# Attention and MLP in one pipeline: transposes of P and the scores moved to the second half of TensorE's slot, with ScalarE's order to match

## Chip, core and metric

The kernel runs on one core of a Trainium2 chip. The metric is the device time of one execution in microseconds. Before the change it is 1642.52 us, the median of three runs (1642.33 to 1642.61). The engines are called PE (TensorE; PEld is its weight load), ACT (ScalarE), DVE (VectorE), POOL (GpSimd) and SP (the engine that issues most DMAs).

## What is computed

Attention in which each row of scores keeps its 32 largest entries, for 8 batches, 8 heads, 576 tokens and a head size of 64; its output, laid out as 4608 tokens by 512, goes through a two-layer MLP with exact gelu. All in fp32.

```python
scores = scale * np.matmul(q, k.transpose(0, 1, 3, 2))
kth = np.partition(scores, -top_k, axis=-1)[..., -top_k:-top_k + 1]
scores = np.where(scores >= kth, scores, -1000000000.0)
scores = scores - np.max(scores, axis=-1, keepdims=True)
attn = np.exp(scores)
attn = attn / (np.sum(attn, axis=-1, keepdims=True) + 1e-09)
x = np.matmul(attn, v)            # then (B,H,S,D) -> (B*S, H*D)
h = x @ w_in                      # 512 -> 2048
g = 0.5 * h * (1.0 + erf(h * inv_sqrt2))
out = g @ w_out                   # 2048 -> 512
```

The weights arrive as 8-byte words, which the kernel turns into fp32 itself in its first slots.

## The kernel before

Instructions are issued to each engine in the order in which the program writes them; no scheduler moves them. So the order is that of one loop, `for n in range(ahead)`, one pass of which is a **slot**. An **item** is 128 rows of scores of two heads (a "pair" of heads); there are 144, 18 to a batch, and the two last row groups of 64 are joined from two pairs ("last" items). The parts of one item are spread over six slots: in slot n the program issues

- `attend(n - 3)` (L509, L520): the product o of the transposed P and v, in every second slot (a **first-layer slot**, by the MLP work that falls into it; the others are **second-layer slots**), and in each slot for last items. Its copy to `xT` on ACT (L514, L524) is put in a list and issued by `copy_x`.
- `softmax(n - 1, e)` for both heads e (L403, L404): a Prelu that pushes entries below the threshold far down, then an exp with its row sum. `add_small` (L396, POOL) follows it.
- `transposes(n - 2)` (L445): 16 transposes of P into two PSUM buffers and two copies `pt` (L457).
- `scores(n + 2)` (L290, L304) with the copy to `s` (L298, L309), and `last_keys(n + 2)` (L323, L331) with the tail transposes of item n - 2 (L462, L467) and their copies (L463, L474, L342, L344).
- `top_k(n)` on DVE (L364, L369): four rounds of eight maxima for both heads. In the third round stands `inverse(n - 1)` (L390), the reciprocal of the row sum, so DVE's top-k of item n can't end before the softmax of item n - 1 has. Then `normalise(n - 1)` (L416, POOL, in some weight slots DVE) and `threshold(n)` (L379, L382, POOL), which gives the next softmax its `neg` and `bias`.
- eight **pieces** of the MLP (`mlp`): a piece is four records of 128x256 matmuls for the first layer (L561, `h_ps`) or two of 128x512 for the second (L597, `y_ps`). Blocks of eight pieces alternate between both layers. The gelus (L572) of a first-layer block are due behind the piece with index `GELU_AT` of the next second-layer block, and are issued at the next `run_gelus()`. A piece is ready only when its tokens are (`ready`): where it isn't, the slot is a **border**, at four slots in every 36.
- pieces of `transpose_qk` (L246): three per pair, of four, two and four transposes of q and k blocks, each with a copy `qk` (L250). The third issues the loads of the pair after next on SP. Slots are given out by `slots_of` and `prep_in`.

Exp and gelu belong to different function tables of ACT; the compiler puts a table load wherever the order changes from one to the other.

PSUM has two buffers with the tag `tp`, taken in turn by everything that is transposed and by o: `tp_qk`, both `tp`, `t_ps`, `o`. `h_ps` has two, `y_ps` two, the scores' `s_ps` one of two banks.

In slots 1 to 10 and 13 to 18 a unit of the weights is made: two or three casts on ACT (L175, L177, L179) at the end of the slot before, sums on POOL (L198, L210, in the later ones also L195). MLP work begins in slot 10 (`START`); before it PE is kept busy with warm matmuls (L675).

Of the kernel before, what the change touches and what calls it, by code (L numbers as in the profile page):

```python
# [14 lines left out]
def kernel(  # L15
# [108 lines left out]
    START = 2 * NP + 2  # L124
# [46 lines left out]
    def weights_size(u):  # L171
        if u not in words:
            return
        w, first, below, d = parts(u)
        nc.scalar.activation(d, first, func=AF.Relu, bias=low, scale=2.0**19)  # L175

        nc.scalar.activation(below, first, func=AF.Prelu, bias=high, scale=2.0**-21, alpha=2.0**40)  # L177
        if not on_pool(u):
            nc.scalar.activation(w.bitcast(i32), w.bitcast(u32), func=AF.Copy, scale=2.0**-13)  # L179

    def on_pool(u):

        return u in words and SLOT_OF[u] > START

    def waits(u):

        return u == ORDER[-1]
# [3 lines left out]
    def weights_add(u):  # L191
        if u in words:
            w, _, below, d = parts(u)
            if on_pool(u):
                nc.gpsimd.tensor_scalar(  # L195
                    w.bitcast(i32), w.bitcast(u32), 2.0**-13, None, op0=ALU.mult
                )
            nc.gpsimd.tensor_tensor(d, d, below, op=ALU.add)  # L198
            if not ends_late(u):
                weights_end(u)  # L200
        made.add(u)

    def ends_late(u):

        return u in words and SLOT_OF[u] <= START

    def weights_end(u):
        if u in words:
            w, _, _, d = parts(u)
            nc.gpsimd.tensor_tensor(d, d, w.bitcast(i32), op=ALU.add)  # L210


    items, starts = [], []
# [20 lines left out]
    def transpose_qk(pair, first=False):  # L234

        rq, rk = raw_of("q", pair), raw_of("k", pair)
        blocks = [(rq, j) for j in range(NJ)] + [(rk, NM)] + [(rk, j) for j in range(NM)]

        def piece(c, n):
            if pair not in qk_of:  # L240
                qk_of[pair] = work.tile([P, KT + SM], f32, tag="qk", bufs=NP + 2, name="qk")
            t = qk_of[pair]
            tp = ps.tile([P, 512], f32, tag="tp", name="tp_qk")
            for x in range(n):
                r, j = blocks[c + x]
                nc.tensor.transpose(  # L246
                    tp[:, x * P : (x + 1) * P], r[:, j].rearrange("p e d -> p (e d)"), ident
                )
            copy = nc.vector.tensor_copy if first and c > 0 else nc.scalar.copy
            copy(out=t[:, c * P : (c + n) * P], in_=tp[:, 0 : n * P])  # L250
            if c == 0:
                load("q", pair + 2)
                load("k", pair + 2)

        return [lambda c=c, n=n: piece(c, n) for c, n in ((6, 4), (4, 2), (0, 4))]
# [5 lines left out]
    def row(i, e):  # L261
        return S_of[i][:, e * S : (e + 1) * S]
# [111 lines left out]
    def threshold(i):  # L374

        if i < 0 or i >= N:
            return
        st = stat_of[i]
        nc.gpsimd.tensor_scalar(  # L379
            st["neg"], st["top"][:, :, 0 :: TOPK - 1], -1.0, None, op0=ALU.mult  # L380
        )
        nc.gpsimd.tensor_tensor(  # L382
            st["bias"], st["neg"][:, :, 0], st["neg"][:, :, 1], op=ALU.subtract
        )

    def inverse(i):
        if i < 0 or i >= N:
            return
        st = stat_of[i]
        nc.vector.reciprocal(st["rden"], st["den"])  # L390

    def add_small(i):
        if i < 0 or i >= N:
            return
        st = stat_of[i]
        nc.gpsimd.tensor_scalar(st["den"], st["den"], 1e-9, None, op0=ALU.add)  # L396

    def softmax(i, e):

        if i < 0 or i >= N:  # L400
            return
        st, s = stat_of[i], row(i, e)
        nc.scalar.activation(s, s, func=AF.Prelu, bias=st["neg"][:, e, 1:2], scale=1.0, alpha=STEEP)  # L403
        nc.scalar.activation(  # L404
            s, s, func=AF.Exp, bias=st["bias"][:, e : e + 1], scale=1.0,
            accum_out=st["den"][:, e : e + 1],
        )

    def normalise(i, on_dve):

        if i < 0 or i >= N:
            return
        st = stat_of[i]
        for e in range(2):
            s = row(i, e)
            (nc.vector if e >= 2 - on_dve else nc.gpsimd).tensor_scalar(  # L416
                s, s, st["rden"][:, e : e + 1], None, op0=ALU.mult
            )
# [64 lines left out]
    def copy_x():  # L483
        while copies:
            copies.pop()()

    n_tok, read = [0], [0]
# [80 lines left out]
    def gelus(us):  # L568
        for u in us:
            _, n, _, nf = units[u]  # L570
            g_of[u] = work.tile([P, nf, n], f32, tag="g", bufs=4, name="g")
            nc.scalar.activation(g_of[u], h_of.pop(u), func=AF.Gelu)  # L572
# [45 lines left out]


    pieces = []  # L620
    GELU_AT = 5

    def block(u, first):

        do, need = (l1_piece, units[u][0] + units[u][1]) if first else (l2_piece, 0)
        return [(need, lambda w=w, x=x: do(w, x)) for w in (u, u + 1) for x in range(4)]
# [3 lines left out]
    def behind(work, x, us):  # L630
        need, f = work[x]
        work[x] = need, lambda: (f(), waiting.append(us))
        return work

    def run_gelus():
        while waiting:
            gelus(waiting.pop(0))

    pieces += behind(block(0, True), 7, (0, 1)) + block(2, True)
    for u in range(2, NU, 2):  # L640
        pieces += behind(block(u - 2, False), GELU_AT, (u, u + 1))
        if u + 2 < NU:
            pieces += block(u + 2, True)
    pieces += block(NU - 2, False)
    done = [0]

    def mlp(n):
        for _ in range(n):
            if done[0] >= len(pieces) or pieces[done[0]][0] > ready[0] or left[0] == 0:
                return  # L650
            pieces[done[0]][1]()
            done[0] += 1
            left[0] -= 1
            if eager[0]:
                run_gelus()


    ready, left = [0], [0]
# [13 lines left out]
    def keep_busy(count, m):  # L672
        warm = ps.tile([P, 512], f32, tag="l1", name="warm")
        for _ in range(count):
            nc.tensor.matmul(warm[:, 0:P], lhsT=m, rhs=m, start=True, stop=True)  # L675
# [17 lines left out]
    prep_in = {}  # L693
    for pair in range(2, n_pairs):
        b, p = divmod(pair, NP)
        for at, piece in zip(first.get(pair, slots_of[b % 2][p]), transpose_qk(pair)):
            prep_in.setdefault(starts[b] + at, []).append(piece)
    ahead = N + 4
    for n in range(ahead):

        left[0] = 4 if n in (START, START + 1) else 8
        eager[0] = n > N
        if not waits(unit_in(n)):
            weights_add(unit_in(n))
        product = attend(n - 3)
        late = n > START
        copy_x()
        for e in range(2):
            softmax(n - 1, e)
        add_small(n - 1)  # L710
        if waits(unit_in(n)):
            weights_size(unit_in(n))
            weights_add(unit_in(n))
        mlp(1 if product else 3)
        if n < START:

            keep_busy((4 if product or n == 0 else 14) * (1 if n < 5 else 2), ident)

        tails = transposes(n - 2)
        scores(n + 2)  # L720
        ready[0] = n_tok[0]
        prep = prep_in.pop(n, [])
        if n == START + 1:

            for piece in prep:
                piece()
            prep = []
        if n < START and product:
            keep_busy(5 if n < 5 else 10, ident)
        mlp(4)  # L730
        last_keys(n + 2, tails)
        if ends_late(unit_in(n)):
            weights_end(unit_in(n))
        for piece in prep:
            mlp(1)
            piece()
        if n == 1:
            keep_busy(8, ident)

        run_gelus()  # L740
        mlp(left[0])
        run_gelus()
        u = unit_in(n + 1)
        if n < N:
            top_k(n, {2: lambda: inverse(n - 1)})
        else:
            inverse(n - 1)

        normalise(n - 1, 2 if on_pool(u) else 0)
        threshold(n)  # L750

        if not waits(unit_in(n + 1)):
            weights_size(unit_in(n + 1))
        for m in (n + 1, n + 2):

            if m > 2 and waits(unit_in(m)) == (m == n + 1):
                load_weights(m)
        if n <= NP:
            load("v", n)
# [38 lines left out]
```

## Time and profile before

| | |
|---|---|
| median of three runs | 1642.52 us |
| the profiled execution | 1642.62 us |
| its span, first to last instruction | 1640.9 us |
| PE matmul busy | 1589.6 us |
| DVE busy | 1412.3 us |
| ACT busy | 1179.4 us |
| POOL busy | 665.4 us |
| mean granted TensorE clock | 0.993 |

The busy time of PE is that of its records, whose ends are modelled, so a wait of PE shows better in the chain and in the waits than in this share. In a line of the waits the columns are: who waited, for whom, us in total, times, longest. In a line of the chain: start, us, what. In a line of the timeline: start, us, engine, line, operation, and in brackets the engine's idle time before it and what ended that. In a line of the stages: busy time of PE, PEld, DVE, ACT and POOL with the number of instructions, then the granted clock, the DMA share and GB/s.

### The profile page before, as it was taken

The page shows a single profiled execution, that of the slowest core. Times are in us where ns is not written, and L with a number is a line of the kernel's source. Part 1 is how long each engine was busy: PE and PEld are TensorE (multiplying, and loading weights), DVE is VectorE, ACT ScalarE, POOL GpSimd, SP SyncE. Part 2 cuts the span into 40 slices and gives each one's busy share as a digit, 9 for nine tenths or more (in the row PEclk, how much of TensorE's full clock was granted, in tenths as well). Part 3 has the DMA queues.
Part 4 walks back from the last instruction along what each step waited for, and adds up shares of the span by engine and source line. Part 5 has one row for each costly group of instructions (what it writes and reads, how often), then busy time and mean ns, then how long its engine had stood idle before and what let it go on. Part 6 is the DMA issues. An engine that isn't in the chain of part 4 may idle for free.

```text
span 1640.9 us, 27895 instructions
## 1 busy us (share of the span) xinstructions
PE 1589.6 (97%) x10336; PEld 1059.6 (65%) x10336; DVE 1412.3 (86%) x3046; ACT 1179.4 (72%) x2132; POOL 665.4 (41%) x760
## 2 busy tenths in 40 slices
PE   7888999999999999999999999999999999999999
PEld 6766566766666666666666656676666656666665
DVE  8998889989899988998999898998989889899800
ACT  6988777777777777777777777777777777777720
POOL 4885744333343333333333333333333333333300
PEclk9999999999999999999999999999999999999999
DMA  6523310011201011011110111001110101000000
GB/s 167 153 75 106 92 43 1 14 29 30 50 1 28 22 38 29 1 28 36 30 28 1 43 30 43 1 14 29 44 36 1 28 16 34 3 7 7 7 14 13
DMA packets 126776, 56.33 MB, mean 34 GB/s; under 512 B 117776, under 2 KB 118064, under 8 KB 126640
## 3 DMA queue, kind: packets, MB, share of 16 engines
q1 hardware_dynamic: 125376, 54.12, 12.3%
q8 instruction: 82, 1.34, 0.3%
q10 hardware_dynamic: 1200, 0.39, 0.1%
q14 instruction: 54, 0.44, 0.1%
q0 software_dynamic: 64, 0.03, 0.0%
HBM read 45.08 MB, written 9.44 MB: 33 GB/s over the span
## 4 chain that ended last, share of the span: by engine, by line
PE 84%; ACT 10%; POOL 3%; issue 1%; DMA 1%; SPq 0%; DVE 0%; ACTq 0%; DVEq 0%; POOLq 0%
PE y_ps L597 31%; PE h_ps L561 31%; PE s_ps L290 6%; PE tp L445 5%; PE o L509 4%; ACT L572 3%; POOL s L416 2%; PE tp_qk L246 2%; PE t_ps L323 2%; ACT g L572 2%; ACT s L404 1%; ACT s L403 1%; PE s_ps L304 1%; PE t_ps L462 1%; ACT qk L250 1%
## 5 line engine op out<-in xcount | busy, mean ns | idle before, releaser
L364 DVE MAX8 top<-rest 128x8 f32<-128x576 f32 x864 | 608.9, 746 | 0.0
L561 PE MATMUL h_ps<-xT,w_in_sb 128*128 128x256 f32 (+1 forms) x2560 | 554.6, 365 | 10.1 <-ACT g L572 9.7
L416 POOL TENSOR_SCALAR s<-s,rden 128x576 f32<-128x576 f32 x278 | 477.5, 1727 | 160.3 <-DVE rden L390 157.9
L597 PE MATMUL y_ps<-w_out_sb,g 128*128 128x512 f32 x1152 | 535.7, 599 | 0.0
L561 PEld LDWEIGHTS h_ps<-xT,w_in_sb 128*128 128x128 f32 x2560 | 434.7, 191 | 102.1 <-ACT g L572 29.1
L369 DVE MATCH_REPLACE8 rest<-top,rest 128x576 f32<-128x576 f32 x576 | 423.1, 742 | 0.0
L597 PEld LDWEIGHTS y_ps<-w_out_sb,g 128*128 128x128 f32 x1152 | 207.3, 190 | 206.9 <-issue 203.2
L396 POOL TENSOR_SCALAR den<-den 128x2 f32<-128x2 f32 x144 | 32.0, 222 | 688.9 <-ACT s L404 688.5
L403 ACT ACTIVATE s<-s,neg 128x576 f32<-128x576 f32 x288 | 222.1, 771 | 85.4 <-POOL neg L379 85.4
L404 ACT ACTIVATE s<-s,bias 128x576 f32<-128x576 f32 x288 | 223.4, 776 | 12.9 <-ACT s L403 0.4
L369 DVE MATCH_REPLACE8 rest<-top,s 128x576 f32<-128x576 f32 x288 | 211.5, 741 | 0.0
L364 DVE MAX8 top<-s 128x8 f32<-128x576 f32 x288 | 201.9, 742 | 0.1
L509 PE MATMUL o<-pt,raw_v 128*64 128x256 f32 x1280 | 154.5, 388 | 1.8 <-ACT qk L250 1.0
L457 ACT COPY pt<-tp 128x512 f32<-128x512 f32 x256 | 135.7, 580 | 17.0 <-PE tp L445 15.7
L390 DVE RECIPROCAL rden<-den 128x2 f32<-128x2 f32 x144 | 22.6, 157 | 142.4 <-POOL den L396 142.1
L445 PEld LDWEIGHTS tp<-ident,s 64*128 64x128 f32 x2304 | 86.0, 139 | 90.2 <-issue 69.2
L290 PE MATMUL s_ps<-qk 64*128 64x256 f32 x1024 | 139.6, 390 | 1.4 <-ACT s L296 0.8
L463 ACT COPY pt<-t_ps 128x128 f32<-128x128 f32 x128 | 34.5, 269 | 140.3 <-PE t_ps L462 139.9
L298 ACT ACTIVATE s<-s_ps 128x1024 f32<-128x1024 f32 x127 | 131.7, 1037 | 2.6 <-PE s_ps L290 2.6
L509 PEld LDWEIGHTS o<-pt,raw_v 128*64 128x64 f32 x1280 | 87.0, 138 | 67.1 <-ACT pt L463 16.7
L445 PE MATMUL tp<-ident,s 64*128 64x64 f32 x2304 | 109.0, 230 | 12.9 <-ACT xT L514 12.2
L572 ACT ACTIVATE g<-h_ps 128x512 f32<-128x512 f32 x144 | 78.6, 595 | 37.8 <-PE h_ps L561 37.1
(77 smaller groups left out, 1220.4 us busy)
## 6 DMA issues: line engine op xcount, KB each, us to landing
raw_q<-in_q_dram SPq DMA_DIRECT2D x64, 128.0 KB, 2.4
raw_v<-in_v_dram SPq DMA_DIRECT2D x64, 128.0 KB, 2.4
raw_k<-in_k_dram SPq DMA_DIRECT2D x62, 128.0 KB, 2.5
out_dram<-y SPq DMA_DIRECT2D x31, 256.0 KB, 2.1
w_out_sb<-in_moe_w_in_dram SPq DMA_DIRECT2D x14, 511.8 KB, 5.0
w_out_sb<-in_moe_w_out_dram SPq DMA_DIRECT2D x10, 511.8 KB, 4.1
words<-in_moe_w_out_dram SPq DMA_DIRECT2D x6, 511.8 KB, 4.3
out_dram<-y SPq DMA_DIRECT2D x9, 128.0 KB, 2.3
```

Source lines behind the costliest of these rows:

```text
L290: nc.tensor.matmul(s_ps[:, e, c * 256 : (c + 1) * 256], lhsT=lhsT[rows, :], rhs=qk[rows, KT + c * 256 : KT + (c + 1) * 256], start=True, s ...
L364: nc.vector.max(st["top"][:, e, 8 * r : 8 * r + 8], cur[e])
L369: nc.vector.match_replace(rest[:, e], st["top"][:, e, 8 * r : 8 * r + 8], cur[e], LOWEST)
L403: nc.scalar.activation(s, s, func=AF.Prelu, bias=st["neg"][:, e, 1:2], scale=1.0, alpha=STEEP)
L404: nc.scalar.activation(s, s, func=AF.Exp, bias=st["bias"][:, e : e + 1], scale=1.0, accum_out=st["den"][:, e : e + 1],)
L416: (nc.vector if e >= 2 - on_dve else nc.gpsimd).tensor_scalar(s, s, st["rden"][:, e : e + 1], None, op0=ALU.mult)
L445: nc.tensor.transpose(tps[g][:, at : at + TL], s[rows, first[e] + j * P : first[e] + (j + 1) * P], ident[rows, rows],)
L457: nc.scalar.copy(out=dst, in_=src)
L509: nc.tensor.matmul(o[e * D : (e + 1) * D, 0:n], lhsT=vt[:, j, e, :], rhs=pt[:, e * NM + j if j < NM else 2 * NM, :], start=(j == 0), stop= ...
L561: nc.tensor.matmul(h_tile(u)[:, i, :], lhsT=w_in_sb[:, ko, f * P : (f + 1) * P], rhs=xT[:, ko, c0 : c0 + n], start=(ko == 0), stop=(ko == ...
L572: nc.scalar.activation(g_of[u], h_of.pop(u), func=AF.Gelu)
L597: nc.tensor.matmul(y_of[sub], lhsT=g_of[u][:, i, sub * P : (sub + 1) * P], rhs=w_out_sb[:, f, :], start=(f == 0), stop=(f == FT - 1),)
```

## The change

The transposes of P and the scores go behind four or five of the slot's pieces of MLP, where one or three pieces stood ahead of them before. On ACT the copy of x goes between the two halves of the softmax, except at a border, where it stays ahead of both. The gelus fall due behind the second piece of a second-layer block, where it was the sixth, so in most second-layer slots they are issued behind the softmax and ahead of the q/k copies. The q/k pieces go ahead of the transposes of P in the slot, and from the second batch on they fall a slot later. `ready` is set at the start of the slot. At a border, and up to slot 10, the q/k pieces are issued ahead of all MLP work. What is computed, the tiles and the buffers stay.

```diff
-    GELU_AT = 5
+    GELU_AT = 1
...
-            prep_in.setdefault(starts[b] + at, []).append(piece)
+            prep_in.setdefault(starts[b] + at + (b > 0), []).append(piece)
...
         late = n > START
+        border = late and done[0] < len(pieces) and ready[0] < pieces[done[0]][0]
+        ready[0] = n_tok[0]
+        if border:
+
+            copy_x()
+        softmax(n - 1, 0)
         copy_x()
-        for e in range(2):
-            softmax(n - 1, e)
+        softmax(n - 1, 1)
         add_small(n - 1)
...
-        mlp(1 if product else 3)
-        if n < START:
-
-            keep_busy((4 if product or n == 0 else 14) * (1 if n < 5 else 2), ident)
-
-        tails = transposes(n - 2)
-        scores(n + 2)
-        ready[0] = n_tok[0]
         prep = prep_in.pop(n, [])
-        if n == START + 1:
-
+        if border or not late:
             for piece in prep:
                 piece()
             prep = []
+        if n < START:
+
+            keep_busy((4 if product or n == 0 else 14) * (1 if n < 5 else 2), ident)
+        mlp(1 if product else 3)
+        run_gelus()
+        mlp(1)
+        for piece in prep:
+            piece()
+            mlp(1)
+        mlp(max(0, left[0] - 4) if late else 0)
+        tails = transposes(n - 2)
+        scores(n + 2)
         if n < START and product:
             keep_busy(5 if n < 5 else 10, ident)
-        mlp(4)
+        mlp(2)
         last_keys(n + 2, tails)
...
-        for piece in prep:
-            mlp(1)
-            piece()
```

## Prediction

> **What bounds the kernel now.** I read the page first (busy shares, the chain), then the waits of the steady stretch from 254 to 1415 us, then the chain of one pair of slots, then the timeline of the first 42 us.
>
> ```profile
> PE 1589.6 (97%) x10336; PEld 1059.6 (65%) x10336; DVE 1412.3 (86%) x3046; ACT 1179.4 (72%) x2132; POOL 665.4 (41%) x760
> ...
> PE 84%; ACT 10%; POOL 3%; issue 1%; DMA 1%; SPq 0%; DVE 0%; ACTq 0%; DVEq 0%; POOLq 0%
> ```
>
> TensorE (PE) is filled nearly throughout, and 84% of the chain is PE. So the change can win only what PE waits for. The waits from 254 to 1415 us say how much that is:
>
> ```profile
> DVE rden L390 <- POOL den L396: 107.6, 54, 3.7
> ...
> ACT s L403 <- POOL neg L379: 62.2, 42, 2.1
> ...
> PE h_ps L561 <- ACT g L572: 8.2, 18, 1.3
> ...
> PE tp L445 <- ACT xT L514: 7.0, 12, 0.8
> ```
>
> Only some 16 us of 1161 are waits of PE. DVE and ACT wait more, but DVE's 9.70 us of work per slot stay below PE's 10.7, so their waits are slack. One of the twelve waits for xT, in the chain:
>
> ```profile
> 807.05 0.45 PE tp_qk L246 x4
> 807.50 0.02 issue
> 807.52 0.59 ACT qk L250
> 808.11 0.02 issue
> 808.12 1.28 ACT L572
> 809.42 1.09 ACT g L572 x2
> 810.50 0.27 ACT xT L514
> 810.78 0.04 issue
> 810.82 0.71 PE tp L445 x15
> ```
>
> PE needs 2.31 us for the product o between 807.5 and 809.8, while ACT copies q and k, loads gelu's table, does two gelus and only then copies o to xT. The second PSUM buffer of the transposes is free after that copy.
>
> **Steady slots, before.** The starts of the transposes, slot by slot in the timeline, give a pair without any wait: 446.22 to 466.69 us, 20.47 us. Its parts are in the chain: transposes 0.64, scores 0.92, last keys and tail 0.33, o 2.31, an MLP piece 0.87 (0.19 more for the first one after scores or o), q/k transposes 0.45 or 0.23. Sums of these, set against the slots, leave these waits per 36 slots (two batches): 0.86, 1.09, 0.86 and 0.54 at the four borders, where PE has no MLP piece between o and the transposes; 0.12 to 0.37 in seven slots where a first-layer piece waits for the gelu behind a q/k copy, 2.25 together; 1.35 once, where two copies of y stand ahead of the gelus. Sum 6.95.
>
> **Steady slots, after.** I write t for the end of PE's tail transpose. ACT's softmax starts at t+0.37 (two small copies) and takes 3.21, or 4.51 with a table load (819.60 to 822.81 and 810.64 to 815.15 us).
> - Second-layer slot with q/k work: softmax to t+3.58, table load to 4.88, gelus and the start of the copy at 5.86, copy done 6.45, PE may go on at 6.49. PE's work up to its transposes: 2 pieces 1.73, 4 pieces 3.44, q/k 0.45, 1 piece 0.86, so 6.48. Wait 0.0, without any margin, 27 times in the three periods.
> - First-layer slot: x is copied from t+3.3 to 3.7, o ends at t+3.17, the q/k copy ends near t+6.2, PE asks at 7.27. Wait 0; the gelus are done a slot ago. The 2.25 go.
> - Border: o ends t+3.17, x copied 3.20 to 3.58, PE's first piece at 3.62, its transposes at 7.08. But the q/k copy now stands behind the whole softmax: 3.45 + 4.51 less 0.09 of overlap = 7.87, done 8.24 or 8.46. PE waits 1.2, 1.42, 1.2; at the fourth border, without q/k work, 0.4 for x. Sum 4.2 against 3.35: the borders get dearer.
> - The slot with two copies of y: x behind gelus, copies and the first half of the softmax, 7.2 against PE's 6.7. Wait 0.5 for 1.35.
>
> Sum 4.7, gain 2.25 per period, 6.75 for three. The stretch from 1415 us on has one border and little else: 0.7 more.
>
> What makes the softmax's start possible: DVE's rden came near t+9.4 in first-layer slots and ACT's next softmax then waited for neg (the 62.2 us above). After, softmax ends near t+5.1, rden at 5.5; POOL's normalise (two of 1727 ns) and neg follow, 4.0 us later, t+9.5. The next softmax wants it at t+11.4: 1.9 us of margin. DVE's 9.70 a slot, 19.4 a pair, fit into 20.5.
>
> What is moved costs nothing by itself: both orders have 136 table loads, equal matmuls and copies. The q/k loads on SP are issued one slot later, up to 11 us; they take 2.4 us to land and are wanted some nine slots on. That cover gone, one slot would wait a few us.
>
> **A rule against it.** The load's row and the chain around it:
>
> ```profile
> L572 ACT ACT_TABLE_LOAD x68 | 87.2, 1283 | 0.6
> ```
>
> The chain shows 0.02 us ahead of it and 0.01 behind, so 1.3 us for a switch. The Trainium skill, ScalarE: Activation LUTs, section "What ACT_TABLE_LOAD costs", gives 2.66 us with a drain of 1.38. By that rule the copy of each tight second-layer slot would come 1.35 us late, 27 x 1.35 = 36 us more in all; the trace decides for 1.3 us.
>
> **The start.** The first slots go at DVE's pace (98.7 us busy from 11 to 110 us), so what delays an early reciprocal is never caught up there.
>
> ```profile
> 18.62 0.63 PE L246 MATMUL tp_qk<-ident,raw_k 128*128 128x128 f32 x4 [2.16 <-DMA raw_k<-in_k_dram]
> ...
> 19.29 0.59 ACT L250 COPY qk<-tp_qk 128x512 f32<-128x512 f32 x1 [2.01 <-PE tp_qk L246]
> ...
> 19.77 1.23 ACT L175 ACTIVATE w_in_sb<-w_out_sb,low 128x1024 int32<-128x1024 int16 x1
> ...
> 23.27 0.76 ACT L403 ACTIVATE s<-s,neg 128x576 f32<-128x576 f32 x1
> ...
> 26.91 0.17 DVE L390 RECIPROCAL rden<-den 128x2 f32<-128x2 f32 x1
> ```
>
> In slot 0 the third pair's k is now transposed ahead of the warm matmuls and the scores, so these wait for the load of k too, which lands at 18.5. Scores then end near 20.7, their two copies (1.02 and 0.27) move from 16.1-17.3 to 20.75-21.8, and weights and softmax follow 2.0 us later. The reciprocal had 0.06 us to spare (9.75 us per slot). **+2.05**; bounds 0 (all hidden) and 2.1.
>
> **The slots with weight casts** (11 to 18). ACT also has two casts, 2.43 us. A second-layer slot has 0.37 + 2.43 + 3.21 + 1.28 + 0.97 + copy, PE goes on at t+8.7 with 6.25 of work (wait 2.45), then t+9.2 with 7.56 (1.65, twice); the first-layer ones wait 0.86 and 1.75. Before, the transposes waited 2.2 and 3.3 in the first-layer ones alone. Before that, q/k copies stand behind softmaxes that wait for DVE (0.9, then 1.7 us of PE). Followed slot by slot at equal MLP work, the new order is behind by 2.2 us at slot 12, 4.6 at 13, 3.2 at 14 and 15, 2.5 at 16 to 18, and, as the gap of 16.02 us between transposes (204.79 to 220.81) shrinks, 1.5 at slot 20. **+1.5**; bounds -3 (the waits of slots 11 to 18 above, 5.5, half saved) and +5 (the 4.6 kept).
>
> A wait also slows PE's clock: behind the wait that ends at 155.47,
>
> ```profile
> 156.00:160.00 4.00, 4.00 (x23) 2.08 (x20) 3.58 (x8) 3.88 (x8) 3.84 (x3) 0.62 0.61 246
> ```
>
> the granted clock (third column from the end) is 0.62, which costs 4 x 0.38 = 1.5 us. Both orders have such waits in these slots; I set them off, and keep 1.5 either way in the bounds.
>
> **Sum.** The profiled execution took 1642.62 us, span 1640.9 and 1.7 around it, against the median of 1642.52. 1642.6 - 6.75 - 0.7 + 2.05 + 1.5 = **1638.7 us**. A measurement tells about 0.2% (3.3 us) from no change; this is just past it.
>
> **Rivals.**
> 1. The borders and weight slots cost less: if the q/k copies at nine borders and the weight slots cost nothing new, 9 x 1.27 = 11.4 less, and with 1.5 + 2.05 still paid 1627; half of it 1632 to 1633. For it: a wait of one buffer leaves every second transpose free. Against: they alternate between both buffers.
> 2. It cancels: the late start and weight slots (3.6, up to 7) take what the steady part wins (7.5). 1642.5. For it: both are sums of waits near 1 us.
> 3. Slower: the q/k copy in the second-layer slots, which has no margin. Every 0.1 us later costs 27 x 0.1 = 2.7 us; 0.15 undoes the forecast, 0.27 makes it slower by 0.2%, and 0.45 gives 1651. For it: before, this softmax waited for neg up to 2.1 us. Against: the 1.9 us of margin.
> 4. The order on the engines does not do what is said: the transposes do move behind four or five pieces and the gelus ahead of the q/k copies in the built order, so no chance is given.
>
> **Chances.** Forecast 0.50 (its own 1635 to 1642: 0.30 faster, 0.20 within 0.2%); rival 1 0.22; rival 2 0.10; rival 3 0.18. Faster 0.52, same 0.30, slower 0.18. The range from 1630 to 1648 leaves out the far halves of rivals 1 and 3.
>
> **What would show it.** Right: waits of h_ps for g gone; waits of tp for xT gone, and instead tp waiting for qk at borders, 1.2 to 1.4 us nine times; softmax without waits for neg in second-layer slots; pairs without q/k work still 20.5; the first reciprocal at 28.9. Wrong: tp waiting for qk in ordinary second-layer slots, DVE filled without gaps, or slots 11 to 18 longer than a hundred us by more than 5.

## The result and the profile after

The changed kernel is slower: **1663.34 us** (median of 4 runs, 1660.59 to 1665.78) against 1642.42 for the kernel before beside it, ratio **1.0127**, 95% interval 1.0109 to 1.0145. The forecast of 1638.7 us and its range up to 1648 missed. The ratios here and below can differ from the quotient of the two medians by 0.1%. The profiled execution took 1664.74 us, span 1663.0, mean granted clock 0.986 (before 0.993).

The lines of the page that answer to those shown of before, busy shares and chain by engine:

```profile
PE 1603.1 (96%) x10336; PEld 1068.6 (64%) x10336; DVE 1411.8 (85%) x3046; ACT 1183.3 (71%) x2132; POOL 664.9 (40%) x760
...
PE 84%; ACT 12%; POOL 2%; issue 1%; DMA 1%; SPq 0%; DVE 0%; ACTq 0%; DVEq 0%; POOLq 0%
```

The same instructions do the same work; PE's records are 13.5 us longer, at a lower granted clock, and ACT has a larger share of the chain. Where the time went shows when both traces are compared **at equal work**: the start of the k-th of the 1152 matmul records of MLP's second layer (L597).

| record | before, us | after, us | after is late by |
|---|---|---|---|
| 1st | 140.23 | 155.20 | 14.97 |
| 65th | 242.75 | 264.07 | 21.32 |
| 833rd | 1269.58 | 1293.01 | 23.43 |
| 1121st | 1623.29 | 1645.42 | 22.13 |

So 15 us are lost in slots 0 to 11, 6 in the slots with weight casts, and from 264 us to the end, 84% of the span, 0.8.

**Steady stretch.** The waits from 254 to 1415 us:

```profile
DVE rden L390 <- POOL den L396: 110.9, 48, 5.3
...
ACT s L403 <- POOL neg L379: 17.8, 18, 1.8
...
PE tp L445 <- ACT qk L250: 11.0, 10, 1.2
...
PE tp L445 <- ACT xT L524: 1.3, 3, 0.5
```

The waits of `h_ps` for the gelu and of `tp` for L514 are gone, and ACT's for neg fell from 62.2 to 17.8. In their place `tp` waits ten times for the copy of q and k, nine of them at borders. The chain of one border:

```profile
749.17 0.87 ACT s L404 x2
750.04 0.27 ACT qk L250
...
750.35 0.70 PE tp L445 x15
```

The copy comes straight behind the softmax, and PE's transposes straight behind the copy. A pair of slots without a wait still takes 20.46 us.

**The start.** The timeline of the first slot:

```profile
18.72 1.09 PE L246 MATMUL tp_qk<-ident,raw_k 128*128 128x128 f32 x4 [4.23 <-DMA raw_k<-in_k_dram]
...
19.60 1.91 PE L675 MATMUL warm<-ident 128*128 128x128 f32 x8
...
21.44 2.05 PE L290 MATMUL s_ps<-qk 64*128 64x256 f32 x8
...
31.79 0.17 DVE L390 RECIPROCAL rden<-den 128x2 f32<-128x2 f32 x1 [4.58 <-POOL den L396]
```

PE stands for 4.23 us on the load of k and then runs at about half rate (scores took 1.13 to 1.14 us elsewhere). The first reciprocal, forecast for 28.9, comes at 31.79. And it isn't the only late one. DVE's waits from 20 to 130 us:

```profile
DVE rden L390 <- POOL den L396: 13.7, 9, 4.6
```

Before, this line was 0.2 us, one wait. 4.58 of the 13.7 are the first slot's; the other eight come later. The 11th reciprocal is at 138.83 us, before at 124.84: 14.0 late, the 4.9 of the first one and 9.1 of the later waits. PE's transposes of P wait in these slots too; from 11 to 132 us, first before, then after:

```profile
PE tp L445 <- ACT xT L514: 1.2, 4, 0.4
```

```profile
PE tp L445 <- ACT qk L250: 8.9, 4, 4.0
PE tp L445 <- ACT xT L514: 7.7, 3, 2.8
```

One slot with a product, ACT, PE and DVE together:

```profile
81.44 0.78 ACT L403 ACTIVATE s<-s,neg 128x576 f32<-128x576 f32 x1 [0.76 <-POOL neg L379]
...
83.08 0.35 ACT L514 COPY xT<-o 128x256 f32<-128x256 f32 x1
...
83.48 0.71 PE L445 MATMUL tp<-ident,s 64*128 64x64 f32 x15 [2.82 <-ACT xT L514]
...
89.50 0.27 ACT L463 COPY pt<-t_ps 128x128 f32<-128x128 f32 x1 [2.61 <-PE t_ps L462]
...
96.97 0.17 DVE L390 RECIPROCAL rden<-den 128x2 f32<-128x2 f32 x1 [1.82 <-POOL den L396]
```

The copy of o now stands behind half a softmax, and that behind neg, that is behind DVE. The transposes wait 2.82 us for the copy; with them scores, warm matmuls and tail transposes come late, ACT waits 2.61 us for these ahead of its casts and the next softmax, and DVE waits for that softmax's sum. Before, the copy stood ahead of both softmax halves, and the transposes of these slots waited 0.4 us at most.

### The profile page after: what moved, and what is told of

Its sections match the earlier page's. It is cut to its first block, busy times and chain, and to the rows that moved or that the text cites. A ratio compares the mean times of both kernels' runs of the same rounds, so it can differ in the third digit from the quotient of the medians.

```text
span 1663.0 us, 27913 instructions
## 1 busy us (share of the span) xinstructions
PE 1603.1 (96%) x10336; PEld 1068.6 (64%) x10336; DVE 1411.8 (85%) x3046; ACT 1183.3 (71%) x2132; POOL 664.9 (40%) x760
## 3 DMA queue, kind: packets, MB, share of 16 engines
q1 hardware_dynamic: 125376, 54.12, 12.2%
## 4 chain that ended last, share of the span: by engine, by line
PE 84%; ACT 12%; POOL 2%; issue 1%; DMA 1%; SPq 0%; DVE 0%; ACTq 0%; DVEq 0%; POOLq 0%
PE y_ps L597 29%; PE h_ps L561 27%; PE o L509 8%; PE s_ps L290 7%; PE tp L445 6%; ACT s L404 3%; ACT s L403 2%; PE t_ps L323 2%; PE tp_qk L246 1%; ACT L404 1%; POOL s L416 1%; PE s_ps L304 1%; PE t_ps L462 1%; PE o L520 1%; ACT w_out_sb L177 1%
## 5 line engine op out<-in xcount | busy, mean ns | idle before, releaser
L597 PE MATMUL y_ps<-w_out_sb,g 128*128 128x512 f32 x1152 | 544.8, 602 | 0.0
L597 PEld LDWEIGHTS y_ps<-w_out_sb,g 128*128 128x128 f32 x1152 | 205.3, 191 | 192.7 <-issue 189.2
L445 PEld LDWEIGHTS tp<-ident,s 64*128 64x128 f32 x2304 | 91.5, 141 | 120.0 <-issue 60.7
L445 PE MATMUL tp<-ident,s 64*128 64x64 f32 x2304 | 117.1, 232 | 41.4 <-ACT qk L250 28.4
L290 PE MATMUL s_ps<-qk 64*128 64x256 f32 x1024 | 148.5, 405 | 1.4 <-ACT s L296 0.8
```

The source lines that it names most:

```text
L290: nc.tensor.matmul(s_ps[:, e, c * 256 : (c + 1) * 256], lhsT=lhsT[rows, :], rhs=qk[rows, KT + c * 256 : KT + (c + 1) * 256], start=True, s ...
L445: nc.tensor.transpose(tps[g][:, at : at + TL], s[rows, first[e] + j * P : first[e] + (j + 1) * P], ident[rows, rows],)
L597: nc.tensor.matmul(y_of[sub], lhsT=g_of[u][:, i, sub * P : (sub + 1) * P], rhs=w_out_sb[:, f, :], start=(f == 0), stop=(f == FT - 1),)
```

## Experiments

**Theory 1**: the order of the slots up to 10 costs some 15 us, slots 11 to 19 some 6, the steady order nothing either way. **Theory 2**: the slots with weight casts are the price. **Theory 3**: the steady order is. All runs, with the difference that the ratio makes of 1642.6 us:

| run | median, us | ratio (95%) | us |
|---|---|---|---|
| after | 1663.34 | 1.0127 (1.0109 to 1.0145) | +20.9 |
| old_to_10 | 1647.48 | 1.0029 (1.0019 to 1.0038) | +4.8 |
| old_to_19 | 1643.80 | 1.0002 (0.9993 to 1.0011) | +0.3 |
| old_from_11 | 1654.76 | 1.0064 (1.0049 to 1.0079) | +10.5 |
| x_first | 1657.73 | 1.0085 (1.0070 to 1.0100) | +14.0 |
| old_slot_0 | 1659.09 | 1.0103 (1.0088 to 1.0118) | +16.9 |
| qk_last | 1656.71 | 1.0084 (1.0067 to 1.0101) | +13.8 |
| both_start | 1651.26 | 1.0053 (1.0038 to 1.0068) | +8.7 |
| warm_first | 1662.43 | 1.0117 (1.0103 to 1.0131) | +19.2 |
| qk_before_softmax | 1647.14 | 1.0027 (1.0016 to 1.0038) | +4.4 |
| x_between | 1630.57 | 0.9926 (0.9912 to 0.9939) | -12.2 |
| after_x_between | 1649.39 | 1.0037 (1.0023 to 1.0050) | +6.1 |
| x_between_10 | 1634.36 | 0.9944 (0.9932 to 0.9957) | -9.2 |
| x_ahead_to_19 | 1634.08 | 0.9942 (0.9929 to 0.9956) | -9.5 |
| x_between_14 | 1629.44 | 0.9913 (0.9898 to 0.9928) | -14.3 |
| x_between_17 | 1631.53 | 0.9930 (0.9917 to 0.9942) | -11.5 |
| qk_before_gelu | 1626.60 | 0.9899 (0.9886 to 0.9913) | -16.6 |

### Which stretch: three mixed orders

The body of the slot, the due time of the gelus and the slot of the q/k pieces were taken from the one kernel or the other by the slot's number.

```diff
+        if n <= START:            # old_to_10; START + 9: old_to_19; n > START: old_from_11
+            (body of the slot as before)
+        else:
             (body of the slot as after)
```

> The slots up to 10 (the start, with the warm matmuls) keep the order of before, with gelu's piece and the q and k work where they were; from slot 11 on the order of after. Theory 1, that the start costs some 15 us (14.97 us late at the first second-layer piece) and slots 11 to 19 some 6: 1663 - 15 = 1648. Theory 2, that the slots with weight casts cost most, the start's delay being swallowed there anyway: 1658 to 1663. Theory 3, that the steady order costs most (borders, q and k copies): 1660 or more. Only theory 1 gives 1645 to 1651.

Measured +4.8, as theory 1 alone said.

> The order of before up to slot 19, that is the start and all slots with weight casts; the order of after from slot 20 on. Theory 1: the start (15) and slots 11 to 19 (6) both go, and what stays is the steady order, which by the waits counted in the trace of after (7.2 us in 36 slots against 6.95) costs 0 to 1 us: 1641 to 1644. Theory 3, steady order dear: over 1650. My forecast's steady gain of 6.75 us would still show here, if it exists and was only covered: 1635 to 1637.

Measured +0.3: the steady order by itself is worth nothing, not the 6.75 us of the forecast, and theory 3 falls. Its difference to the run before, 4.5 us (about 2 either way by the intervals), is the price of slots 11 to 19. The two profiled executions don't show it: that of `old_to_10` is the fastest of its ten (1644.91 us), that of `old_to_19` the slowest (1645.73).

> The reverse: the order of after up to slot 10, the order of before from slot 11 on. Theory 1: the start alone costs 15 us: 1655 to 1659. Theory 2: the start's delay is swallowed by the gaps of slots 11 to 18, as the order of before has gaps there of its own: 1643 to 1648. Theory 3: 1643 to 1646.

Measured +10.5, a little below theory 1's band by the ratio, at its edge by the median; theory 2 falls. Start 10.5 ahead of the old order and 16.1 (20.9 - 4.8) ahead of the new one: some 5 us (about 4 either way by the intervals) are paid only where a late start meets the new order in the slots with casts.

### What in the start

```diff
 x_first                             | qk_last, in slots 0 to 10
-        if border:                  | -            piece()      (behind the softmax)
+        if border or not late:      | +            mlp(1)
             copy_x()                | +            piece()      (at the slot's end)
```

`both_start` has both edits; `old_slot_0` has the body of before for `n < 1`.

> After, with one thing put back: up to slot 10 the copies of o to xT stand ahead of the softmax again, not between its halves. Theory 1 says that in these slots the copy waits behind a softmax that waits for DVE, that TensorE's transposes wait for the copy (8.2 us in four waits) and that this makes about half of the start's loss: 1655 to 1658. A rival inside theory 1, that the start's loss is the wait for the first load of k and the slow clock behind it, and that the rest only follows from those: 1661 to 1663.

Measured +14.0, so 6.9 us from the place of the copy of o, as the theory said. DVE's waits up to the 11th reciprocal fall from 13.7 to 10.5, the first (5.0) still among them. So not all of it is won there: at equal work the profiled executions are 3.4 us apart at the first second-layer record and 6.0 at the 65th.

> After, with slot 0 alone in the order of before: the third pair's k is transposed behind the warm matmuls and the scores again, so TensorE doesn't stand for 4.23 us on its load. If this wait and the slow clock behind it (scores in 2.05 us, 1.13 before; first reciprocal 4.88 us late) are kept by all that follows: 1663.3 - 4.9 = 1658.5. If the later slots' own waits swallow it, 1661 to 1663. If the first delay is also what makes the later ones, more than 7 us: below 1656.

Measured +16.9, 4.0 us from slot 0: most of it is kept. The first reciprocal is at 27.06, 4.7 us earlier, and the 11th still 3.3 us; but 10.5 us of waits remain in the later slots.

> After, with the transposes and copies of q and k put back to the end of the slot in slots 0 to 10; the copy of o stays between the softmax halves and the transposes of P stay in the second half. This takes away the wait for the first load (4.9) and the four waits of the transposes for the copy of q and k (8.9 us, partly beside DVE's waits). If the start's loss is half from the place of x (5.6 us measured) and the rest from the place of q and k: 1663.3 - 5 to 9 = 1654 to 1658. If the rest is from the transposes of P coming late in the slot by themselves: 1660 or more.

Measured +13.8, 7.1 us from the place of q and k, four of them slot 0's; DVE's waits up to the 11th reciprocal are 6.2.

> The two put back together in slots 0 to 10: the copy of o ahead of the softmax, q and k at the slot's end. If x's place and q and k's place make the start's loss between them: 1647 to 1650, as with the whole old order up to slot 10 (1647.5). If the transposes of P behind the scores' slot and gelu's place matter by themselves: 1652 to 1656.

Measured +8.7, between the two bands (median 1651.26 us); 12.2 us come from the two together. DVE's waits are 0.36 us and the 11th reciprocal is at 124.85 (before 124.84): the two edits put DVE's start back completely. What is left against `old_to_10`, 3.9 us, is mostly one wait of 4.70 us in slot 11 (at 125.03), where the transposes stand on a q/k copy behind a softmax that had waited 3.96 us for neg; the first second-layer record is 2.9 us later than there.

### The wait for the load and the clock

```diff
+        if n == 0:
+            keep_busy(17, ident)
         for piece in prep:
             piece()
...
-        if n < START:
+        if 0 < n < START:
...
```

> After, with slot 0's warm matmuls ahead of its transposes of q and k, and 17 of them in place of 4 (34 records of some 0.12 us, 4.0 us, where TensorE stood for 4.23 us). The wait for the load of k stays; the idle time goes. My forecast of the start took the wait but full-rate matmuls behind it: the first reciprocal at 28.9 us. After shows it at 31.79. If the 2.4 us between (8 warm matmuls 1.91 us, scores 2.05 in place of 1.13) are the clock's answer to the idle time and the warm matmuls' place: first reciprocal at 28.7 to 29.2, scores in 1.1 to 1.2 us, and 1660 to 1661 in all. If the slow matmuls have another cause (the table of code loading, the transfers): scores again near 2 us, the reciprocal at 30.5 or later, 1662 to 1663.

The timeline of this kernel, scores and first reciprocal:

```profile
19.26 1.14 PE L290 MATMUL s_ps<-qk 64*128 64x256 f32 x8
...
28.70 0.17 DVE L390 RECIPROCAL rden<-den 128x2 f32<-128x2 f32 x1 [1.84 <-POOL den L396]
```

The load of k still lands when it did (PE's transposes at 18.70), with 0.77 us of idle time in place of 4.23, and everything behind it runs at full rate. Of the 3.1 us by which the reciprocal is earlier, some 2.2 are the rate (warm matmuls 0.98, scores 0.91, transposes 0.32) and 0.9 the eight warm matmuls that no longer stand between load and scores. So the forecast had sized the wait about rightly (with the eight matmuls back in their place the reciprocal would be near 29.6, for its 28.9) and left out the clock. The total gains less than the expected 2 to 3 us by the ratio: +19.2 against +20.9, intervals overlapping, 2.0 us at equal work in the profiled executions. The lead is 3.6 us at the sixth reciprocal and 2.2 from the seventh on, which waits 3.13 us for its softmax (1.82 in after).

### Why the steady order gained nothing

```diff
 qk_before_softmax (from slot 20)    | x_between (from slot 20)
         if border:                  | -        if border:
             copy_x()                | -            copy_x()
+            (q/k pieces)            |          softmax(n - 1, 0)
         softmax(n - 1, 0)           |          copy_x()
```

> The order of before up to slot 19, then the order of after, with one change: at the borders the transposes and copies of q and k stand behind the copy of o and ahead of the softmax, not behind it. Theory: what took the steady gain are the ten waits of the transposes for the copy of q and k at the borders (11.0 us from 254 to 1415 us), and nothing else is late there: 1643.8 - 10 = 1633 to 1635. Rival: ScalarE's queue is only reordered, so the wait comes back at another place, for P's copies or the gelus, since the softmax now starts 0.6 us later: 1641 to 1644.

Measured +4.4: 4 us worse than with q and k behind the softmax, so the rival holds, and more. Border and next slot in its timeline:

```profile
343.90 0.78 ACT L403 ACTIVATE s<-s,neg 128x576 f32<-128x576 f32 x1 [1.48 <-POOL neg L379]
...
350.13 0.71 PE L445 MATMUL tp<-ident,s 64*128 64x64 f32 x15 [1.53 <-ACT qk L250]
```

The border's wait is gone (1.46 us at equal work), but its softmax and reciprocal are no earlier while PE is; the next softmax waits for neg, and the copy of q and k of that slot, behind it, comes too late. There 1.6 us are lost again in six of nine places, 1.8 in two and 3.4 in one: 16.6 for the 13.1 that the borders win.

> The order of before up to slot 19, then the order of after without its exception for borders: there too the first half of the softmax stands ahead of the copy of o. In the trace of the kernel with the old order up to 19, ScalarE stands for 2.73 us on o at a border, though its softmax could start; half of a softmax with its table load takes 2.9 us, so the copy starts some 0.1 to 0.3 us later than now, and the whole softmax and the copy of q and k end 2.6 us earlier. Theory: the border's dear part is this idle time of ScalarE; nine waits of 1.2 to 1.45 us go, three to nine waits of 0.3 us for x come: 1643.8 - 11 + 2 = 1635 (1633 to 1637), and the next slot's softmax starts no later than now, so that no new wait comes there. Rival: DVE and GpSimd set the pace through neg around the borders, as in the kernel with q and k ahead of the softmax: 1642 to 1645.

Measured **-12.2**, better than the theory's band. In the kernel with the old order up to 19 a border looked like this, first ACT, then PE:

```profile
338.69 0.37 ACT L514 COPY xT<-o 128x256 f32<-128x256 f32 x1 [2.73 <-PE o L509]
...
343.85 0.70 PE L445 MATMUL tp<-ident,s 64*128 64x64 f32 x15 [1.18 <-ACT qk L250]
```

ACT stood for 2.73 us on o with a softmax it could have begun. Without the exception (ACT's timeline, then the waits from 254 to 1415 us):

```profile
334.48 0.35 ACT L514 COPY xT<-o 128x256 f32<-128x256 f32 x1
...
336.32 0.35 ACT L250 COPY qk<-tp_qk 128x256 f32<-128x256 f32 x1
```

```profile
PE tp L445 <- ACT qk L250: 0.2, 1, 0.2
```

Half a softmax fits into that time, the copy follows it without a pause, and q and k are copied some 2.8 us earlier against PE's transposes. At equal work each of the nine borders gains 1.46 us, 13.1 in all; so a border whose wait is listed with 1.18 us costs 1.46.

> After, with nothing changed but the exception for borders taken out: start and slots with weight casts as in after. If the nine steady borders are worth 1.46 us each whatever the start was: 1663.3 - 13.1 = 1650.2, less up to 1 for the border in slots 11 to 19. If part of that gain was only there because of the earlier start: 1653 or more.

Measured +6.1, 14.8 us less than after: the 13.1 come whatever the start was, and the border among slots 11 to 19 adds some.

### The slots with weight casts

```diff
 x_between_10, _14, _17:  old order for n <= START, START + 4, START + 7
 x_ahead_to_19 (on x_between_10)     | qk_before_gelu (on x_between_10)
+        if n <= START + 9:          | -        if border or not late:
+            copy_x()                | +        if border or n <= START + 9:
         softmax(n - 1, 0)           |              (q/k pieces behind the softmax)
```

> The same without the exception for borders, but with the order of before only up to slot 10, so with slots 11 to 19 (the weight casts) in the new order too. If these slots lose by the waits for q and k at their border as well, the distance to the kernel with the old order up to 19 shrinks from the 3.7 us between the two kernels with the exception to about 1: 1635 to 1637. If the casts are what makes these slots dear, it stays 3 to 4: 1638 to 1640, under theory 1.

Measured -9.2, below both bands, but 3.0 us (by the medians 3.8) worse than with the old order up to 19; the intervals overlap, the ranges of the two sets of five runs don't. So the price isn't the border's exception.

> The kernel with the order of before up to slot 10 and no exception for borders behind it (1634.4), with one edit: in slots 11 to 19 the copy of o stands ahead of the softmax. Its trace loses 3.22 us to the kernel with the old order up to 19 in one slot: GpSimd has three weight operations (7.8 us) ahead of the normalisation, neg comes 6.29 us late, the first half of the softmax waits for it with the copy of o behind, and the transposes wait 2.22 us for this copy. Theory: that wait is the price of the slots with weight casts: 1634.4 - 2 to 3.5 = 1631 to 1632.4. Rival: the waits for the copy of q and k in the same slots (7.3 us in eight waits) are the price, and the copy ahead makes the borders there dearer: 1634 to 1636.

Measured -9.5: nothing gained; the theory that blamed the longest wait falls. At equal work 2.5 us are won where that wait was, but 2.8 had been lost ahead of it and 1.5 are lost again behind it. So the wait for neg looks like the visible end of a delay, not its cause; the next two runs bear that out.

> As the kernel without the exception for borders (1630.6 with the order of before up to 19, 1634.4 with it up to 10), with the order of before up to slot 14. If slots 11 to 14 make the loss (transposes waiting 0.5, 2.3, 0.7 and 1.5 us for q and k there): 1631. If it is made later, where DVE's pace first differs (the reciprocals come at 198.7 and 198.4 us in the two traces, and then at 208.4 and 211.0): 1634.

> The same with the order of before up to slot 17. If the loss is made in slots 15 to 17, 1630.6 to 1631.5; if it is made in slots 18 and 19, where the softmax waits 6.29 us for neg, 1633.5 to 1634.5.

Measured -14.3 and -11.5: neither loses to `x_between` (-12.2). With the old order up to 14 the new one does no harm in slots 15 to 19, though a softmax waits 6.28 us for neg there, as in `x_between_10` (6.29). So the loss comes from the order of slots 11 to 14. That rests on `x_between_14`: the interval of `x_between_17` (0.9917 to 0.9942) reaches that of `x_between_10` (0.9932 to 0.9957).

> The kernel without the exception and with the order of before up to slot 10 (1634.4), with the transposes and copies of q and k of slots 11 to 19 straight behind the softmax, ahead of gelu's table load and two gelus (2.4 us). In its trace the transposes of P wait 7.3 us in eight places for these copies. If those waits are the price of the slots with weight casts: 1630.6 to 1632. If DVE's pace through rden and neg is the price: 1633.5 to 1635.

Measured **-16.6**, below both bands and the fastest kernel of this study, 7.8 us below `x_between_10` and 36.7 below after by the medians. The waits from 132 to 254 us, first of `x_between_10`, then of this one:

```profile
PE tp L445 <- ACT qk L250: 7.3, 8, 2.3
```

```profile
PE tp L445 <- ACT qk L250: 4.2, 5, 1.7
```

The waits fall by 3.1 us, and DVE's loop gains twice that: its 20th reciprocal comes at 233.1 us, 239.3 in `x_between_10`. The place of q and k behind a table load and two gelus was the price of these slots. With q and k ahead of them, the new order even wins some 4 us there against the old one (1626.6 to 1630.6, intervals that just touch). Three things stay open. The edit moves the transposes of q and k on PE with their copies. Up to the 15th reciprocal (172.2 us) both kernels agree within 0.1 us, so what is won shows only in slots 16 to 20, behind the slots that made the loss. And the granted clock differs: in the profiled execution of `x_between_10` it is 0.83 from 200 to 210 us and again from 220 to 230, together 3.4 us of clock, and 1.00 here; all five of its runs have 0.992 to 0.994 over the span, all four here 0.995 to 0.998. Whether the clock follows from the shorter waits, and how much of the 6.2 us is the clock's, was not taken apart.

## Why the prediction was wrong

**The start** (+2.05, bounds 0 and 2.1) is the step that failed: 16.1 us measured in front of the new order, 14.97 at equal work in the profiled execution. At equal work the other terms are 6.35 for +1.5 in the slots with casts, +1.9 for -6.75 in the steady ones and -1.0 for -0.7 behind them, so the start is half of the whole miss. The forecast rightly saw that TensorE would wait for the load of k and that DVE could not catch up. It then took the start to be that one delay. Two things were left out. The clock: it counted a slow clock for the slots with casts, but sized the matmuls behind this wait at full rate; 2.2 us, as `warm_first` shows. And, much larger, slots 2 to 10 were not stepped through: there the copy of o and the copies of q and k stand behind a softmax that waits for DVE, PE's transposes wait for both (7.7 and 8.9 us), and the loop comes back to DVE late, by 1.7 to 2.0 us in four of these slots and by less in four more, 9.1 us in all. The upper bound of 2.1 was no bound, since it covered only the edit that had been looked at.

**Steady slots** (-6.75 in three periods): +1.9 at equal work from the 65th to the 961st record, and with the last stretch +0.3 by the ratio of `old_to_19`. Of the mechanisms most were right: the seven first-layer waits and most of the waits for xT went, the borders got waits for q and k, pairs without waits stayed at 20.5. Mis-sized were small terms: a border costs 1.46 where the listed wait is 1.2; the second-layer slots "without any margin" wait 0.15 us or less (their 16 transposes start within 0.70 us, for 0.55 elsewhere), one of them 0.4; the slot with two copies of y waits some 0.7 for 0.5. A period (288 records) takes 387.5 to 387.8 us for 387.0 before, so that by the forecast's own count of 6.95 it waits some 7.6 us for the forecast's 4.7; what the rest of it is was not taken apart. The forecast accepted the borders' 4.2 as given, though its rival 1 priced them at 11.4 in all; they were the whole gain, and 12 to 13 us were to be had there.

**The last stretch** (-0.7): right; 1.0 us is won at equal work between records 961 and 1121, in after as in `old_to_19`.

**Slots with weight casts** (+1.5, bounds -3 and +5): 4.5 behind the old start, 6.4 behind the new one. The bounds held the first; the mean was mis-sized because the q/k copies behind gelu were followed as waits of single slots, while `qk_before_gelu` shows DVE's loop gaining twice what their waits fall by. The lower bound rests on a misreading: the waits of 2.2 and 3.3 us that the forecast gives for the transposes of before are 1.8 and 1.7 in its trace (at 155.47 and 182.27).

**Rivals.** Slower was given 0.18, with the second-layer q/k slots as its mechanism. The sign came, the mechanism not: those slots make 2.5 us a period at most (7.6 less three borders of 1.46 and the 0.7). Rival 1, cheaper borders, became true only in `x_between`.

**The rule against it.** After's group of loads:

```profile
L572 ACT ACT_TABLE_LOAD x68 | 87.2, 1283 | 1.1
```

Here the trace decides once more against 2.66 us for a switch (the Trainium skill, ScalarE: Activation LUTs, section "What ACT_TABLE_LOAD costs"): with it each of 27 second-layer slots would have waited 1.35 us, and they wait 0.15 or less, one of them 0.4.

**Open.** Why a late start and the new order of slots 11 to 19 together cost some 5 us more than each by itself was not taken apart. The best order of slots 0 to 10 was not looked for beyond the old one.

## What to carry to other kernels

In an engine with one queue, a copy that frees a buffer inherits every wait of what stands ahead of it: before moving it behind another operation, ask what that operation waits for in each stage, the first slots above all, where another engine sets the pace. Size a moved step in every stage by walking its loop once around (here PE, ACT, GpSimd, DVE and back), since a delay on the engine that sets the pace is kept. And look for idle time ahead of a copy on its own engine: half a softmax put into ACT's 2.73 us turned a change worth nothing into one worth 12.

## What the runs showed of the hardware

After 4.23 us without work, 8 warm matmuls took 1.91 us, 0.24 each, and scores 2.05; with 0.77 us of idle time the 34 warm ones ahead took 3.96 us, 0.12 each, and scores 1.14. The Trainium skill (TensorE: Matmul & The Clock Gate, section "Part 1: The HAM clock gate (the "warmup" mystery)") gives half rate after an idle window of some 3.4 us, and the two waits lie on either side of that. The granted clock shows the same: in after it is 0.50 from 16.6 to 23.3 us, in `warm_first` 1.00 from 17 to 23. But a shorter wait can slow it too: in after the clock falls some 2 us into the wait of 4.23 (1.00 from 14.5 to 16.5 us), and after the 2.82 us ahead of 83.48 it is 0.50 from 84.8 to 88.1: the 20 warm matmuls at 85.25 took 3.88 us, 0.19 each, and the 56 at 89.30 ran at 0.11 again.
